# Setting the sign of converted float64 weights with one 16-bit and/or on the vector engine

## The chip, the core and the metric

The kernel runs on one core of a Trainium2 chip. The metric is device time in microseconds. The core has five engines with an instruction queue each: PE (matmul; its weight loads have a queue of their own in the profile, PEld), DVE (the vector engine), ACT (the scalar engine), POOL and SP. SP only issues DMAs here.

## The reference

Three stages follow each other on a batch of 2 with 768 positions: banded attention with 8 heads of 64, a token and channel mixer with skip connections, and a gated layer with a spatial mix.

```python
x = _attn_ref(...)                       # (2, 768, 512)
h = np.maximum(x.T @ w_tok1, 0.0) @ w_tok2          # per batch, over positions
u = x + h.T
x = u + np.maximum(u @ w_ch1, 0.0) @ w_ch2
h = np.maximum(x @ w_in, 0.0); u, v = split(h)
v = (v - mean(v)) / sqrt(var(v) + 1e-6)
y = (u * (w_spatial @ v + b_spatial)) @ w_out
```

All weights but `w_spatial` arrive as float64: a product of float32 draws with a numpy double.

## The kernel before

No engine reads float64, so the kernel loads the raw 8 bytes of each weight and rebuilds its value on the chip. That is done by `weight` (line 366), in blocks of 128 partitions by 512 weights. There are 42 such blocks: 6 for the token mixer (`tok_weights`, tile `wt`), 24 for the channel mixer (`ch_weight`, two for each of 12 slices `j`), 8 for `w_in` and 4 for `w_out` (`mlp2_weights`). `w_spatial` is float32 and takes a shorter way.

For each block the steps are these. Line 389 loads the block on SP's queue into a `raw` buffer, of which there are two. `mid` is a view of the middle 32 bits of each weight and `top` a view of its top 16 bits (sign, exponent and the first bits of the mantissa); both step by 8 bytes from one weight to the next. On ACT, line 390 copies `top` scaled by a power of two into the 16-bit tile `c` (its first half, `pw`), and line 391 writes the sign of `top` (1 or -1) into the second half of `c` (`sg`). On DVE, line 392 shifts the bits of `pw` by three and clears the sign bit, line 394 multiplies `pw` by `sg`, line 395 cuts `pw` to a power of two (`qq`), line 397 scales `mid` by `qq`, and line 399 adds `pw`. The result is split into a high part rounded to fp32r (line 400, a copy that either ACT or DVE may do) and a low rest (line 401, DVE). Every product of the mixers is then three fp32r matmuls (`mm3`, line 342).

The order of all instructions is made by `Plan` (line 98) when the kernel is built. Each operation names the engines on which it may run with an estimated cost (`act(n)`, `dve(n, x)`, where x is the number of elements per cycle that is assumed); the planner places the operation that can start first, among these the one with the longest chain behind it, and a copy goes to the engine on which it would end first, with a surcharge on busy engines. So a changed cost or a removed operation can change the order on every engine. Each queue then runs in the planned order.

Through attention the planner also places 80 matmuls on zeros (line 598), which occupy PE while it has nothing else. They are always 80, whatever else changes.

The attention groups (`group`, line 518) run scores on PE (line 484), bias and row minimum on DVE (line 501), the exponential on ACT (line 505), transposes on PE (line 511), copies out of PSUM (line 349) and the products with v (lines 539 and 549). The token mixer (`tok`, line 716) needs the `wt` blocks: the first three for its first product, the last three for its second, whose transposes are line 743. The channel mixer (`ch`, line 774) uses `w`, and its slices' weights stay resident for both batches.

Of the kernel before, what the change touches and what calls it, by code (L numbers as in the profile page):

```python
# [10 lines left out]
I16 = mybir.dt.int16  # L11
I32 = mybir.dt.int32
U32 = mybir.dt.uint32
AF = mybir.ActivationFunctionType
ALU = mybir.AluOpType
# [48 lines left out]
def f32(ap):  # L64
    return ap.bitcast(F32)
# [32 lines left out]
class Plan:  # L98
# [13 lines left out]
    def op(self, where, fn, reads=(), writes=(), pri=None, mode="full"):  # L112
        o = Op(where, fn, self.pri if pri is None else pri, len(self.ops))
        o.mode = mode if where[0][0] == "PE" else None
        o.plan, o.lam = self, self.lam
        for key in reads:
            w, r = self.seen.setdefault(key, [[], []])
            o.deps.update(w)
            r.append(o)
            if isinstance(key[0], Buf):  # L120
                key[0].users.append(o)
        for key in writes:
            w, r = self.seen.setdefault(key, [[], []])
            o.deps.update(r)
            o.deps.update(w)
            self.seen[key] = [[o], []]
            if isinstance(key[0], Buf):
                key[0].users.append(o)
                if key[0].first is None:
                    key[0].first = o  # L130
        o.deps.discard(o)
        self.ops.append(o)
        return o
# [65 lines left out]
def act(n, extra=0.0):  # L199
    return ("ACT", n / 1200 + 0.07 + extra)  # L200


def dve(n, x=1):
    return ("DVE", n * 0.00104 / x + 0.07)
# [6 lines left out]
def dma(nbytes):  # L211
    return ("SP", max(nbytes / 400e3, 0.5))
# [73 lines left out]
class Arm:  # L286
# [79 lines left out]
    def weight(self, hi, lo, src, hk, lk):  # L366

        op, n = self.plan.op, src.shape[-1]
        if src.dtype == F32:
            w = self.buf(self.stgp, "raw", [P, 1032], F32, 2)
            op([dma(P * n * 4)], lambda e: self.SY.dma_start(w()[:, :n], src), [], [(w,)])
            self.split(hi, lo, lambda: w()[:, :n], n, (w,), hk, lk)
            return
        w = self.buf(self.stgp, "raw", [P, 1032], I32, 2)
        c = self.buf(self.stgp, "c", [P, 1024], BF16, 2)  # L380
        q = self.buf(self.stgp, "q", [P, 512], BF16, 2)
        a = self.buf(self.stgp, "a", [P, 512], F32, 2)
        V = self.V
        mid = lambda: w()[:, 1:1 + 2 * n:2].bitcast(U32)
        top = lambda: w().bitcast(BF16)[:, 4:4 + 4 * n:4]
        pw, sg, qq = (lambda: c()[:, :n]), (lambda: c()[:, 512:512 + n]), (lambda: q()[:, :n])
        i16 = lambda x: x().bitcast(I16)
        aa = lambda: a()[:, :n]
        op([dma(P * n * 8)], lambda e: self.SY.dma_start(w().bitcast(I16)[:, 1:1 + 4 * n], src.bitcast(I16)), [], [(w,)], LDP)
        op([act(n)], lambda e: self.SC.mul(pw(), top(), 2.0 ** -112), [(w,)], [(c, 0)])  # L390
        op([act(n)], lambda e: self.SC.activation(sg(), top(), AF.Sign), [(w,)], [(c, 1)])  # L391
        op([dve(n, 2)], lambda e: V.tensor_scalar(
            out=i16(pw), in0=i16(pw), scalar1=3, scalar2=0x7FFF, op0=ALU.logical_shift_left, op1=ALU.bitwise_and), [], [(c, 0)])
        op([dve(n, 2)], lambda e: self.tt(e, pw(), pw(), sg(), ALU.mult), [(c, 1)], [(c, 0)])
        op([dve(n, 2)], lambda e: V.tensor_scalar(
            out=i16(qq), in0=i16(pw), scalar1=-128, scalar2=None, op0=ALU.bitwise_and), [(c, 0)], [(q,)])
        op([dve(n)], lambda e: V.scalar_tensor_tensor(  # L397
            out=aa(), in0=mid(), scalar=2.0 ** -36, in1=qq(), op0=ALU.mult, op1=ALU.mult), [(w,), (q,)], [(a,)])
        op([dve(n)], lambda e: self.tt(e, aa(), aa(), pw(), ALU.add), [(c, 0)], [(a,)])
        op(self.copies(n), lambda e: self.copy(e, hi(), aa()), [(a,)], [hk])  # L400
        op([dve(n)], lambda e: self.tt(e, lo(), aa(), f32(hi()), ALU.subtract), [(a,), hk], [lk])
# [645 lines left out]
```

## Time and profile before

| what | value |
|---|---|
| median of 3 runs | 476.6 us (476.33 to 477.08) |
| the profiled execution | 476.65 us |
| its span, first to last instruction | 474.9 us |
| outside the span | 1.75 us |
| PE busy | 469.1 us (99%) |
| PE weight loads busy | 414.3 us (87%) |
| DVE busy | 291.0 us (61%) |
| ACT busy | 210.3 us (44%) |

The busy share of an engine counts the time in which at least one of its instructions is under way. Matmuls overlap, and their ends are modelled, so short gaps between them can be covered. The weight loads are a second, stricter look at the same engine. Attention ends on PE at about 103 us, the token mixer's last part and the channel mixer of the first batch follow, the channel mixer of the second batch runs to about 336 us, and the gated layer fills the rest.

### The profile page before, as it was taken

How to read it: one execution, taken by the hardware profiler on the slowest of the kernel's cores; microseconds unless marked ns; L12 is line 12 of the kernel's file. 1: busy time of each engine (PE TensorE's matmuls, PEld its weight loads, DVE VectorE, ACT ScalarE, POOL GpSimd, SP SyncE). 2: the span in 40 equal slices, each digit the busy share in tenths (PEclk: the TensorE clock that was granted, in tenths of full speed). 3: DMA queues.
4: the chain of work that ended last, by engine and by line, in shares of the span. 5: the costliest groups of instructions: out<-in, count | busy, mean ns of one | idle time of the engine just before them, and what ended most of it. 6: DMA issues, size and time to landing. Idle time of an engine off the chain costs nothing.

```text
span 474.9 us, 8988 instructions
## 1 busy us (share of the span) xinstructions
PE 469.1 (99%) x3557; PEld 414.3 (87%) x3557; DVE 291.0 (61%) x781; ACT 210.3 (44%) x531; POOL 7.8 (2%) x17
## 2 busy tenths in 40 slices
PE   9999999999999999999999999999999999999996
PEld 5887888899988888888888888888999988899985
DVE  4899999979988787113977833247942503722520
ACT  5998899974645564101435311123612122411121
POOL 0111010000000000000000000000000000000000
PEclk9999999999999999999999999999999999999999
DMA  7955749223242433000043302110000021000012
GB/s 261 391 212 209 282 159 342 78 94 127 101 169 94 160 109 132 0 1 1 3 149 115 123 33 68 33 35 0 2 0 2 0 81 53 1 0 1 0 46 95
DMA packets 12000, 44.65 MB, mean 94 GB/s; under 512 B 1456, under 2 KB 1968, under 8 KB 10928
## 3 DMA queue, kind: packets, MB, share of 16 engines
q1 hardware_dynamic: 11952, 44.01, 26.0%
q8 instruction: 30, 0.49, 0.4%
q14 instruction: 18, 0.15, 0.1%
HBM read 40.86 MB, written 3.15 MB: 93 GB/s over the span
## 4 chain that ended last, share of the span: by engine, by line
PE 98%; DMA 1%; DVE 0%; issue 0%
PE p L344 27%; PE p L345 27%; PE p L346 27%; PE p L484 4%; PE p L511 4%; PE p L539 3%; PE p L598 2%; PE p L549 1%; DMA raw<-in_qkv 1%; PE p L743 1%; PE p L572 1%; PE dummy L259 1%; DVE c L349 0%; DVE zero L251 0%; DVE shift L253 0%
## 5 line engine op out<-in xcount | busy, mean ns | idle before, releaser
L344 PE MATMUL p<-raw,w 128*128 128x512 f32 (+1 forms) x192 | 64.8, 337 | 0.0
L345 PE MATMUL p<-raw,w 128*128 128x512 f32 (+1 forms) x192 | 64.7, 337 | 0.0
L346 PE MATMUL p<-raw,w 128*128 128x512 f32 (+1 forms) x192 | 64.6, 336 | 0.0
L790 ACT ACTIVATE raw<-p 128x512 fp32r<-128x512 f32 (+1 forms) x48 | 23.6, 491 | 85.1 <-PE p L346 78.3
L791 DVE SCALAR_TENSOR_TENSOR raw<-p,raw 128x512 fp32r<-128x512 f32 (+1 forms) x48 | 26.2, 554 | 35.4 <-ACT raw L790 35.0
L505 ACT ACTIVATE e<-e,nm 128x192 f32<-128x192 f32 (+1 forms) x96 | 42.4, 455 | 4.3 <-DVE nm L501 4.3
L346 PE MATMUL p<-uy1h,w 128*128 128x512 f32 (+2 forms) x128 | 43.2, 337 | 0.0
L346 PE MATMUL p<-uy0h,w 128*128 128x512 f32 (+2 forms) x128 | 43.2, 337 | 0.0
L345 PE MATMUL p<-uy1l,w 128*128 128x512 f32 (+2 forms) x128 | 43.1, 337 | 0.0
L345 PE MATMUL p<-uy0l,w 128*128 128x512 f32 (+2 forms) x128 | 43.1, 337 | 0.0
L344 PE MATMUL p<-uy1h,w 128*128 128x512 f32 (+2 forms) x128 | 43.1, 337 | 0.0
L344 PE MATMUL p<-uy0h,w 128*128 128x512 f32 (+2 forms) x128 | 43.1, 337 | 0.0
L390 ACT ACTIVATE c<-raw 128x512 bf16<-128x512 bf16 x42 | 28.6, 680 | 28.3 <-DMA raw<-in_w_in 12.6
L346 PEld LDWEIGHTS p<-raw,w 128*128 128x128 f32 x192 | 36.1, 188 | 4.2
L344 PEld LDWEIGHTS p<-raw,w 128*128 128x128 f32 x192 | 36.1, 188 | 4.1
L345 PEld LDWEIGHTS p<-raw,w 128*128 128x128 f32 x192 | 36.1, 188 | 4.0
L501 DVE CUSTOM_DVE_ANT_0 e<-p,bias 128x192 f32<-128x192 f32 (+1 forms) x96 | 27.5, 341 | 6.2 <-PE p L484 6.1
L397 DVE SCALAR_TENSOR_TENSOR a<-raw,q 128x512 f32<-128x512 uint32 x42 | 28.8, 686 | 0.4
L355 DVE TENSOR_TENSOR a<-a,c 128x512 f32<-128x512 f32 x42 | 28.8, 686 | 0.2
L391 ACT ACTIVATE c<-raw 128x512 bf16<-128x512 bf16 x42 | 28.3, 673 | 0.0
L355 DVE TENSOR_TENSOR w<-a,w 128x512 fp32r<-128x512 f32 x36 | 24.6, 685 | 2.8 <-ACT w L349 2.7
L355 DVE TENSOR_TENSOR c<-p,bsp 128x384 f32<-128x384 f32 x16 | 8.9, 558 | 28.1 <-PE p L346 28.1
(153 smaller groups left out, 1072.6 us busy)
## 6 DMA issues: line engine op xcount, KB each, us to landing
raw<-in_wch SPq DMA_DIRECT2D x24, 512.0 KB, 3.7
raw<-in_qkv SPq DMA_DIRECT2D x7, 1088.0 KB, 8.6
raw<-in_qkv SPq DMA_DIRECT2D x7, 848.0 KB, 6.3
raw<-in_w_in SPq DMA_DIRECT2D x8, 512.0 KB, 3.8
raw<-in_wt SPq DMA_DIRECT2D x6, 512.0 KB, 7.4
out<-a SPq DMA_DIRECT2D x11, 256.0 KB, 2.0
raw<-in_w_sp SPq DMA_DIRECT2D x6, 384.0 KB, 2.9
raw<-in_w_out SPq DMA_DIRECT2D x4, 512.0 KB, 3.9
```

The lines of the kernel that those rows point to most:

```text
L344: T.matmul(o, lhsT=w[0], rhs=x[0], start=first, stop=False)
L345: T.matmul(o, lhsT=w[0], rhs=x[1], start=False, stop=False)
L346: T.matmul(o, lhsT=w[1], rhs=x[0], start=False, stop=last)
L355: self.eng[e].tensor_tensor(out=o, in0=a, in1=b, op=op)
L390: op([act(n)], lambda e: self.SC.mul(pw(), top(), 2.0 ** -112), [(w,)], [(c, 0)])
L391: op([act(n)], lambda e: self.SC.activation(sg(), top(), AF.Sign), [(w,)], [(c, 1)])
L397: op([dve(n)], lambda e: V.scalar_tensor_tensor(out=aa(), in0=mid(), scalar=2.0 ** -36, in1=qq(), op0=ALU.mult, op1=ALU.mult), [(w,), (q,) ...
L484: T.matmul(banks[k][i]()[x * D:x * D + D, o:o + w], lhsT=r[:, q0:q0 + D], rhs=r[:, k0:k0 + w], start=True, stop=True)
L501: op([dve(w)], lambda e, j=j, o=o, w=w, bs=bs: V.tensor_tensor_reduce(out=e_()[:, o:o + w], in0=s()[:, o:o + w], in1=bias()[:, bs], scale= ...
L505: op([act(w, 0.2)], lambda e, j=j, o=o, w=w: SC.activation(e_()[:, o:o + w], e_()[:, o:o + w], AF.Exp, bias=nm()[:, j:j + 1], scale=-1.0, ...
L790: op([act(n)], lambda e, m=m, r=r, sl=sl, n=n: SC.activation(r()[:, 0, sl], m()[:, :n], AF.Relu), [(m,)], [(r, z, 0)])
L791: op([dve(n)], lambda e, m=m, r=r, sl=sl, n=n: V.scalar_tensor_tensor(out=r()[:, 1, sl], in0=m()[:, :n], scalar=0.0, in1=f32(r()[:, 0, sl] ...
```

## The change

The sign is no longer computed on ACT. Line 391 (Sign, ACT) and line 394 (16-bit multiplication, DVE) go. One DVE instruction takes their place: it masks the sign bit of `top` and joins it to `pw` with an or, both as 16-bit integers. Its first input is the strided view `top`, so it reads the `raw` buffer. The planner is told one element per cycle for it (`dve(n)`), where the multiplication stood with two (`dve(n, 2)`). The second half of `c` is not used any more.

```diff
-        pw, sg, qq = (lambda: c()[:, :n]), (lambda: c()[:, 512:512 + n]), (lambda: q()[:, :n])
+        pw, qq = (lambda: c()[:, :n]), (lambda: q()[:, :n])
         i16 = lambda x: x().bitcast(I16)
         aa = lambda: a()[:, :n]
         op([dma(P * n * 8)], lambda e: self.SY.dma_start(w().bitcast(I16)[:, 1:1 + 4 * n], src.bitcast(I16)), [], [(w,)], LDP)
         op([act(n)], lambda e: self.SC.mul(pw(), top(), 2.0 ** -112), [(w,)], [(c, 0)])
-        op([act(n)], lambda e: self.SC.activation(sg(), top(), AF.Sign), [(w,)], [(c, 1)])
         op([dve(n, 2)], lambda e: V.tensor_scalar(
             out=i16(pw), in0=i16(pw), scalar1=3, scalar2=0x7FFF, op0=ALU.logical_shift_left, op1=ALU.bitwise_and), [], [(c, 0)])
-        op([dve(n, 2)], lambda e: self.tt(e, pw(), pw(), sg(), ALU.mult), [(c, 1)], [(c, 0)])
+        op([dve(n)], lambda e: V.scalar_tensor_tensor(
+            out=i16(pw), in0=top().bitcast(I16), scalar=-32768, in1=i16(pw), op0=ALU.bitwise_and, op1=ALU.bitwise_or), [(w,)], [(c, 0)])
         op([dve(n, 2)], lambda e: V.tensor_scalar(
             out=i16(qq), in0=i16(pw), scalar1=-128, scalar2=None, op0=ALU.bitwise_and), [(c, 0)], [(q,)])
```

## Rows read from the trace of the kernel before

**Rows 1.** The page's first lines and its clock row (40 slices of the span):
```profile
span 474.9 us, 8988 instructions
PE 469.1 (99%) x3557; PEld 414.3 (87%) x3557; DVE 291.0 (61%) x781; ACT 210.3 (44%) x531; POOL 7.8 (2%) x17
...
PEclk9999999999999999999999999999999999999999
```

**Rows 2.** Busy time by stretch: from:to and length, engines, clock, DMA share, GB/s:
```profile
5.00:47.00 42.00, 41.64 (x675) 33.17 (x673) 35.40 (x159) 38.37 (x139) 5.45 (x9) 1.00 0.75 283
47.00:107.00 60.00, 59.51 (x855) 53.31 (x856) 56.00 (x207) 54.31 (x174) 2.14 (x4) 1.00 0.52 191
107.00:190.00 83.00, 83.00 (x488) 73.74 (x487) 69.50 (x151) 44.21 (x80) 0.00 (x0) 1.00 0.38 128
...
230.00:280.00 50.00, 50.00 (x289) 43.72 (x288) 38.75 (x80) 19.03 (x35) 0.00 (x0) 1.00 0.30 100
280.00:470.00 190.00, 190.00 (x1012) 173.41 (x1011) 77.12 (x150) 46.13 (x89) 0.00 (x0) 1.00 0.07 24
```
The engines stand in the order PE, PEld, DVE, ACT, POOL, each with its number of instructions.

**Rows 3.** The chain that ended last, shares of the span by engine (page, 4):
```profile
PE 98%; DMA 1%; DVE 0%; issue 0%
```

**Rows 4.** Groups of instructions by line: busy us, mean ns of one, idle before them:
```profile
L391 ACT ACTIVATE c<-raw 128x512 bf16<-128x512 bf16 x42 | 28.3, 673 | 0.0
L355 DVE TENSOR_TENSOR c<-c 128x512 bf16<-128x512 bf16 x42 | 17.9, 425 | 2.0 <-ACT c L391 1.7
L397 DVE SCALAR_TENSOR_TENSOR a<-raw,q 128x512 f32<-128x512 uint32 x42 | 28.8, 686 | 0.4
L355 DVE TENSOR_TENSOR a<-a,c 128x512 f32<-128x512 f32 x42 | 28.8, 686 | 0.2
```

**Rows 5.** Line 391 alone by stretch: ACT busy, instructions, clock, DMA, GB/s:
```profile
5.00:47.00 42.00, 3.44 (x5) 1.00 0.75 283
47.00:107.00 60.00, 6.30 (x9) 1.00 0.52 191
107.00:190.00 83.00, 13.21 (x20) 1.00 0.38 128
...
230.00:280.00 50.00, 5.30 (x8) 1.00 0.30 100
```

**Rows 6.** Groups by line, 47 to 107 us: the DVE's casts of converted blocks:
```profile
L349 DVE CAST w<-a 128x512 fp32r<-128x512 f32 x4 | 1.7, 418 | 0.0
L349 DVE CAST wth<-a 128x512 fp32r<-128x512 f32 x3 | 1.3, 419 | 0.0
```

**Rows 7.** Groups by line, 5 to 107 us: PE's weight loads and fill:
```profile
L511 PEld LDWEIGHTS p<-ident,e 128*128 128x128 f32 x144 | 15.9, 140 | 4.3 <-ACT pt L349 1.2 <-ACT e L505 1.1 <-ACT ct L349 0.6
L484 PEld LDWEIGHTS p<-raw 64*64 64x64 f32 x336 | 11.0, 132 | 3.7 <-DMA raw<-in_qkv 0.8 <-PE p L572 0.6 <-PE p L511 0.5
...
L598 PE MATMUL p<-zero 128*128 128x256 bf16 x80 | 12.4, 277 | 0.1
```

**Rows 8.** Who waited for whom, 107 to 190 us: total us, times, longest:
```profile
ACT w L349 <- DVE a L355: 14.5, 12, 1.5
...
DVE c L355 <- ACT c L391: 1.2, 5, 0.3
```

**Rows 9.** Timeline around the token mixer's sixth block: start, us, engine, line:
```profile
60.85 0.68 DVE L355 TENSOR_TENSOR wtl<-a,wth 128x512 fp32r<-128x512 f32 x1
...
61.05 0.49 PE L743 MATMUL p<-ident,xp 128*128 128x128 f32 x3
...
61.55 0.33 PE L345 MATMUL p<-wtl,hh 128*128 128x384 f32 x1
```

**Rows 10.** Timeline: PE's longest idle time in attention, before a score group:
```profile
47.49 0.78 PE L484 MATMUL p<-raw 64*64 64x128 f32 x16 [0.62 <-DMA raw<-in_qkv]
```

**Rows 11.** Timeline: both blocks of channel slice 2 written; the slice's first matmul:
```profile
105.91 1.29 DVE L355 TENSOR_TENSOR w<-a,w 128x512 fp32r<-128x512 f32 x2
...
122.32 0.39 PE L344 MATMUL p<-uy0h,w 128*128 128x512 f32 x1
```

## The prediction

> **What bounds the kernel now.** I read the busy shares first. PE is busy for 469.1 of 474.9 us, and its granted clock is full in every slice, so no clock level is to be won or lost [rows 1]. Then I read the chain that ended last: 98% of it is PE [rows 3]. A busy PE can hide gaps, since matmul ends are modelled, so I went on to busy time by stretch [rows 2], cut where the work changes: the first part of attention (5 to 47 us), attention with the token mixer (47 to 107), the channel mixer with most weight conversions (107 to 190), the conversions for the gated layer (230 to 280), and what follows. In the last three PE is busy for the whole stretch while DVE has 13.5, 11.3 and 112.9 us to spare. In the first two PE is still busy for all but 0.36 and 0.49 us, but DVE (35.4 of 42, 56.0 of 60) and ACT (38.4 of 42, 54.3 of 60) are nearly full as well. These are the only stretches in which the two engines that the change touches could set PE's pace.
>
> How much idle time can PE be hiding there? Its weight loads are the stricter measure. They are busy for 73.74 of 83 us, 0.89, in the stretch from 107 to 190, where PE has no gap at all; 0.89 (53.31 of 60) from 47 to 107; and 0.79 (33.17 of 42) from 5 to 47 [rows 2]. If 0.89 is what a full PE looks like, the first stretch hides about 0.1 x 42 = 4.2 us and the second about none. Shapes differ between stretches, so that is an estimate. In the first stretch PE also runs the 80 matmuls on zeros [rows 7]: their number is fixed, so they are work that no faster engine removes.
>
> The Trainium skill (Trainium Kernel Development and Optimization, section Performance Expectations) calls matmul busy time a bad metric because matmuls are pipelined, and wants weight-load busy time read instead. By the first, 99% leaves nothing to gain; by the second, 87% leaves something. The trace sides with the page for the stretch up to 47 us and shows no difference between the second and the third.
>
> **The change part by part.**
>
> *Line 391 goes from ACT.* 42 x 673 ns = 28.3 us of ACT work [rows 4]. By stretch it is 3.44, 6.30, 13.21 and 5.30 us [rows 5]. In the last two ACT is busy for 44.2 of 83 and 19.0 of 50 us, so there the removal is worth nothing: PE is full, and ACT itself waits for DVE (the high cast waited 14.5 us in total for the sum on DVE) [rows 2, 8]. In the first two it takes 9.7 us off an ACT that is busy for 92.7 of 102 us.
>
> *Line 394 becomes the and/or on DVE.* The multiplication takes 425 ns [rows 4]. The trace has no 16-bit and/or with two sources. Its nearest row is line 397: the same instruction kind, the same 512 elements, a first input that steps by 8 bytes in the same buffer, a 16-bit second one: 686 ns [rows 4]. The other end is 425 ns, if the 16-bit form ran as fast as the multiplication that it replaces. I take 686, since the stride is what the two share. So each block costs DVE 0 to 0.26 us more, and I take 0.26: 5 x 0.26 = 1.3 us from 5 to 47, 9 x 0.26 = 2.3 from 47 to 107, 20 x 0.26 = 5.2 from 107 to 190, 8 x 0.26 = 2.1 from 230 to 280; 42 x 0.26 = 11 us in all. DVE's idle time in these stretches is 6.6, 4.0, 13.5 and 11.3 us [rows 2], so it stays under full in each: 36.7 of 42, 58.3 of 60, 74.7 of 83, 40.9 of 50.
>
> The DVE's microarchitecture page of the Trainium skill (Vector Engine (DVE) Microarchitecture Reference, section 5.2) speaks against the change: a source that hops at every element streams at 1.73 ns per column plus about 75 ns, which for 512 columns gives 0.96 us as an estimate, and 0.54 us more per block. This trace disagrees for line 397, which hops by 8 bytes and takes 686 ns, exactly as long as the sum of line 399 without a hop [rows 4].
>
> *What gives DVE the room back.* From 47 to 107 us DVE also does seven casts of high parts (4 and 3, 418 and 419 ns) that may run on either engine [rows 6]. With ACT relieved of 6.3 us there, the planner can move them: up to 7 x 0.42 = 2.9 us off DVE, against the 2.3 us added. If it moves none, DVE keeps 1.7 us of idle time in 60; that is the thin place.
>
> *Waits.* The DVE's wait for the Sign goes (1.2 us from 107 to 190 [rows 8]); late next is line 392's input from line 390, which is untouched. The new instruction waits for the `raw` buffer's load, which line 390 has waited for already, so no new wait stands in DVE's queue. The `raw` buffer is given back by line 397, as before, now 0.26 us later in a block's chain; behind that on SP stand the next weight loads and attention's loads. A conversion that ends later matters only if PE is near it. For the channel slices it is not: slice 2, with the smallest lead, is written by 107.2 and first used at 122.32 [rows 11]; 14 blocks at 0.26 us make it at most 3.7 us later, and the lead stays above 11 us.
>
> *The sum.* 0 us from 107 us on, since PE is full and the weights lead. Before that, a gain or loss only through PE's small waits. The waits that ACT ends at the transposes (line 511) are 1.2 + 1.1 + 0.6 = 2.9 us [rows 7]; these can shrink. PE's longest wait, 0.62 us, is for a load of attention's own and stays [rows 10]. Against this stands the longer DVE chain. The balance is a few tenths down: the profiled execution's 476.65 becomes about 476.4. Its span of 474.9 plus 1.75 us outside is that 476.65, 0.05 above the median of 476.6, so the same number serves for both.
>
> **The rivals.**
>
> *Faster: ACT was pacing attention.* For it: ACT is 91% busy over the first 102 us, and transposes wait for it. Against it: the idle time is partly filled by the fixed matmuls on zeros, so a shorter chain only moves them. If half of the 2.9 us goes the time is 475.2; if all of it, 473.8; an outer bound is the 4.2 us of hidden idle time, 472.5.
>
> *Slower: the sixth token block comes late.* The last low part of `wt` runs from 60.85 to 61.53; PE starts the transposes of the token mixer's second product at 61.05 and the matmul that reads that low part at 61.55 [rows 9]. There is no lead. Six blocks with 0.26 us more each make it 1.6 us later if DVE, which has little room there, does not take the casts off. From the point where PE has no other product ready at 61 us, it waits: 476.65 + 1.6 = 478.2. Against it: the planner knows the longer cost and has attention work to put ahead.
>
> *The order alone.* Removing 42 operations and changing 42 costs lets the planner reorder everything up to 107 us, with no trend. The transposes' weight loads have 4.3 us of idle time in front and the scores' 3.7 [rows 7]; an eighth of these 8 us either way is 1.0 us: 475.6 to 477.6. This mixes into all the cases.
>
> *The change does not do what it says:* the and/or costs DVE nothing (425 ns). Then the slower case falls away and the time is as forecast, 476.4. By the page's 0.96 us per instruction the stretch from 47 to 107 would need 9 x 0.54 = 4.9 us more of a DVE with 4.0 idle. As a mechanism of this kernel, a DVE that is full there delays attention by what does not fit: 56.0 + 4.9 - 60 = 0.9 us, 477.5, unless the casts move. I give it 0.03, within the slower case, because the row of line 397 contradicts it.
>
> **How the numbers follow.** About 0.2% (0.95 us) is what a measurement of this kernel can tell from no change. PE full with waits that cancel (the forecast, the cheap and/or with it): 0.45. Faster, ACT's relief: 0.30. Slower, DVE's chain: 0.25, of which 0.03 is the page's. The range must leave out no more than a fifth: downwards it stops just above the full 2.9 us at 474.0, leaving out the hidden 4.2 us; upwards it takes the 478.2 of the late block and half a microsecond of order on top, 478.8. The likeliest case's own range is 475.6 to 477.6.
>
> **What would show it.** The new DVE row should read close to 686 ns and line 391 should be gone. From 47 to 107 us ACT should lose some 3 to 6 us and DVE stay within 1.5 us of its 56.0, with fewer of the seven casts on DVE. PE should be busy without a gap from 107 us on, and the weight loads from 5 to 107 us keep their idle time to within a microsecond. The forecast is wrong if the idle time at the transposes shrinks by more than a microsecond without appearing elsewhere, if the first matmul of the token mixer's second product waits for `wtl`, or if the channel mixer starts more than 1 us earlier or later than now.

## The result and the profile after

The changed kernel takes 482.7 us (481.68 to 483.42) against 476.8 (476.33 to 477.08): 1.0107 times as long, 95% interval 1.0087 to 1.0127. (The quotient of the two medians is a little larger, 1.0123; shares below go by the ratio.) The profiled execution took 482.98 us, its span is 481.1 us, 6.2 longer than before [rows 1]. The page's first lines, its clock row and its chain of work that ended last, after:

```profile
span 481.1 us, 8908 instructions
...
PE 472.4 (98%) x3557; PEld 416.9 (87%) x3557; DVE 300.9 (63%) x778; ACT 190.8 (40%) x492; POOL 6.9 (1%) x17
...
PEclk9999979999999999999999999999999999999999
...
PE 90%; DMA 3%; DVE 3%; ACT 2%; issue 1%; ACTq 0%; DVEq 0%
```

ACT lost 19.5 us of work and DVE gained 9.9, as the change says; three copies moved from DVE to ACT (DVE 781 to 778 instructions, ACT 531 to 492 with 42 Signs gone). But one slice of the clock row now reads 7, and the chain, 98% PE before [rows 3], holds DMA, DVE and ACT. The price of the new instruction isn't the reason. The groups by line, after (line 393 is the and/or, line 397 the unchanged scaling of `mid`):

```profile
L393 DVE SCALAR_TENSOR_TENSOR c<-raw,c 128x512 int16<-128x512 int16 x42 | 28.9, 688 | 0.3
L397 DVE SCALAR_TENSOR_TENSOR a<-raw,q 128x512 f32<-128x512 uint32 x42 | 28.8, 686 | 0.3
```

Where the time went shows in the busy time by stretch, after (from:to and length; PE, PEld, DVE, ACT, POOL; clock, DMA share, GB/s), beside [rows 2]:

```profile
5.00:47.00 42.00, 41.67 (x654) 33.84 (x654) 34.73 (x155) 37.97 (x137) 4.53 (x9) 1.00 0.72 272
47.00:107.00 60.00, 56.58 (x795) 49.50 (x797) 53.26 (x195) 47.99 (x160) 2.14 (x4) 0.94 0.51 183
107.00:190.00 83.00, 83.00 (x545) 74.17 (x540) 73.72 (x148) 34.77 (x65) 0.00 (x0) 1.00 0.37 127
230.00:280.00 50.00, 50.00 (x288) 43.73 (x288) 44.58 (x88) 15.09 (x26) 0.00 (x0) 1.00 0.27 87
...
280.00:470.00 190.00, 190.00 (x1013) 173.42 (x1012) 80.33 (x156) 45.95 (x89) 0.00 (x0) 1.00 0.07 24
```

From 107 us on PE is full, as before. Only the second stretch is worse: PE is busy for 56.58 us where it was busy for 59.51, and the mean clock is 0.94. A landmark, one product found in both traces, confirms that all of the loss lies early. The first product of the channel mixer for the second batch starts here, before and then after:

```profile
210.17 0.39 PE L344 MATMUL p<-uy1h,w 128*128 128x512 f32 x1
```

```profile
216.36 0.39 PE L344 MATMUL p<-uy1h,w 128*128 128x512 f32 x1
```

From it to the end of the span both kernels take 264.7 us (474.9 - 210.17 and 481.1 - 216.36). The 6.2 us were all lost before it. This is the place, in the timeline after (start, duration, engine, line, [idle before <- what ended it]):

```profile
57.47 0.63 ACT L730 ACTIVATE hh<-p 128x256 fp32r<-128x256 f32 x2
...
60.78 0.65 ACT L390 ACTIVATE c<-raw 128x512 bf16<-128x512 bf16 x1 [2.69 <-DMA raw<-in_wch]
61.34 0.35 ACT L349 COPY ct<-p 128x256 f32<-128x256 f32 x1
...
61.75 0.69 PE L572 MATMUL p<-ident,ct 128*128 128x128 f32 x2 [2.60 <-ACT ct L349]
...
62.37 1.56 PE L484 MATMUL p<-raw 64*64 64x192 f32 x16
```

ACT waits 2.69 us for the load of the seventh weight block, the first of the channel mixer. Behind that step in ACT's queue stands the copy `ct` of attention, and PE needs it: 2.60 us idle. In the kernel before ACT came to the same step after that copy, at a time when the block was there:

```profile
61.99 0.72 ACT L390 ACTIVATE c<-raw 128x512 bf16<-128x512 bf16 x1
```

SP issued the load at 51.49 us, hardly later than before (51.32), behind two loads of attention. The DMA issues from 48 to 56 us give KB and us from issue to landing, before and then after:

```profile
raw<-in_qkv SPq DMA_DIRECT2D x1, 1088.0 KB, 8.8
raw<-in_qkv SPq DMA_DIRECT2D x1, 848.0 KB, 6.5
raw<-in_wch SPq DMA_DIRECT2D x1, 512.0 KB, 8.1
```

```profile
raw<-in_qkv SPq DMA_DIRECT2D x1, 1088.0 KB, 9.8
raw<-in_qkv SPq DMA_DIRECT2D x1, 848.0 KB, 7.5
raw<-in_wch SPq DMA_DIRECT2D x1, 512.0 KB, 9.3
```

So it landed at about 59.4 us before and 60.8 after, while ACT was ready for it at 58.1 (60.78 - 2.69). About half of ACT's wait is thus a load that landed 1.4 us later; with the landing of before it would have been some 1.3 us. Why the three loads took longer isn't shown. As this idle time ended, PE's clock fell to half, 1.2 of 2.4 GHz. Busy time after, cut there:

```profile
57.00:61.30 4.30, 2.15 (x46) 1.84 (x46) 3.04 (x14) 1.61 (x7) 0.00 (x0) 1.00 0.49 165
61.31:68.14 6.83, 6.39 (x35) 5.11 (x35) 4.83 (x18) 6.09 (x21) 0.00 (x0) 0.50 0.02 7
68.20:72.00 3.80, 3.80 (x80) 3.39 (x80) 3.12 (x15) 2.82 (x10) 0.45 (x1) 1.00 0.30 63
```

The sum of the loss: PE is busy for 2.9 us less from 47 to 107 us (59.51 - 56.58), and the 6.39 us of work at half clock would take 3.2 us less at full. Together 6.1 of the 6.2 us. In the trace that accounts for the time. Whether the order or the new work made it so is what the experiments were for.

### The profile page after: what moved, and what is told of

Its sections match the earlier page's. It is cut to its first block, busy times and chain, and to the rows that moved or that the text cites. A ratio compares the mean times of both kernels' runs of the same rounds, so it can differ in the third digit from the quotient of the medians.

```text
span 481.1 us, 8908 instructions
## 1 busy us (share of the span) xinstructions
PE 472.4 (98%) x3557; PEld 416.9 (87%) x3557; DVE 300.9 (63%) x778; ACT 190.8 (40%) x492; POOL 6.9 (1%) x17
## 4 chain that ended last, share of the span: by engine, by line
PE 90%; DMA 3%; DVE 3%; ACT 2%; issue 1%; ACTq 0%; DVEq 0%
PE p L344 26%; PE p L345 26%; PE p L346 26%; DMA raw<-in_wch 3%; PE p L484 3%; PE p L511 3%; PE p L598 2%; PE p L539 2%; PE p L549 1%; PE p L572 1%; PE p L743 1%; ACT e L505 1%; PE dummy L259 1%; DVE xl L355 1%; DVE e L501 0%
## 5 line engine op out<-in xcount | busy, mean ns | idle before, releaser
L390 ACT ACTIVATE c<-raw 128x512 bf16<-128x512 bf16 x42 | 28.2, 674 | 33.9 <-DMA raw<-in_w_in 15.3
L393 DVE SCALAR_TENSOR_TENSOR c<-raw,c 128x512 int16<-128x512 int16 x42 | 28.9, 688 | 0.3
L345 PEld LDWEIGHTS p<-uy1l,w 128*128 128x128 f32 x128 | 24.1, 188 | 2.3
```

The lines of the kernel that those rows point to most:

```text
L345: T.matmul(o, lhsT=w[0], rhs=x[1], start=False, stop=False)
L393: op([dve(n)], lambda e: V.scalar_tensor_tensor(out=i16(pw), in0=top().bitcast(I16), scalar=-32768, in1=i16(pw), op0=ALU.bitwise_and, op1= ...
```

## The experiments

The *cost* theory: the and/or makes each block's DVE chain longer, and that costs the time. The *order* theory: the planner, told other work, emitted another order, and in that order ACT met a load that was not there. The planned orders of the two kernels differ on PE, ACT and DVE: from 5 to 47 us, for one, PE runs 675 matmuls before [rows 2] and 654 after. Ratios are to the kernel before, run beside each experiment, with 95% intervals; they are not the quotients of the medians, from which they differ by up to 0.16 percentage points.

**The new work in the old order.** The and/or runs on the chip, but the planner still counts a Sign (which issues nothing) and the old cost. Against the changed kernel:

```diff
         op([act(n)], lambda e: self.SC.mul(pw(), top(), 2.0 ** -112), [(w,)], [(c, 0)])
+        op([act(n)], lambda e: None, [(w,)], [(c, 1)])
...
-        op([dve(n)], lambda e: V.scalar_tensor_tensor(
-            out=i16(pw), in0=top().bitcast(I16), scalar=-32768, in1=i16(pw), op0=ALU.bitwise_and, op1=ALU.bitwise_or), [(w,)], [(c, 0)])
+        op([dve(n, 2)], lambda e: V.scalar_tensor_tensor(
+            out=i16(pw), in0=top().bitcast(I16), scalar=-32768, in1=i16(pw), op0=ALU.bitwise_and, op1=ALU.bitwise_or), [(c, 1)], [(c, 0)])
```

> The and/or is executed, but the planner still counts a Sign on ACT and the half-cost multiplication, so every queue keeps the order of the kernel before, with the Sign left out and the and/or in the multiplication's place. Order theory (the loss comes from one conversion step placed ahead of attention's copies on ACT, where it waits for its load, and from the halved clock behind that): no such wait here, 476.0 to 477.6 us, granted clock full from 7 to 470 us. Cost theory (the and/or takes 688 ns on DVE where the multiplication took 425, and DVE paces PE before 107 us): 480 us or more, with PE's idle time spread over 47 to 107 us.

Measured: 478.4 against 477.7 us, 1.0021 (1.0007 to 1.0034). Clock full, span 476.6 us. Its busy time by stretch, and the group of its and/or (line 394 here):

```profile
47.00:107.00 60.00, 58.73 (x870) 52.21 (x865) 57.10 (x207) 49.34 (x163) 2.15 (x4) 1.00 0.56 200
107.00:190.00 83.00, 83.00 (x489) 73.90 (x488) 74.47 (x152) 34.68 (x62) 0.00 (x0) 1.00 0.37 127
```

```profile
L394 DVE SCALAR_TENSOR_TENSOR c<-raw,c 128x512 int16<-128x512 int16 x42 | 29.0, 691 | 0.3
```

All the new work costs 0.2%, about a fifth of the loss. DVE rises to 57.1 of 60 us, yet PE shows no wait for it: its longest, before 107 us, is 1.0 us for a load of attention's, where it was 0.62 [rows 10].

**The old work in the new order.** The Sign is issued in the same step as the scaled copy, and the multiplication stands where the and/or stands, at its planned cost.

```diff
-        op([act(n)], lambda e: self.SC.mul(pw(), top(), 2.0 ** -112), [(w,)], [(c, 0)])
-        op([act(n)], lambda e: self.SC.activation(sg(), top(), AF.Sign), [(w,)], [(c, 1)])
+        op([act(n)], lambda e: (self.SC.mul(pw(), top(), 2.0 ** -112), self.SC.activation(sg(), top(), AF.Sign)), [(w,)], [(c, 0)])
...
-        op([dve(n, 2)], lambda e: self.tt(e, pw(), pw(), sg(), ALU.mult), [(c, 1)], [(c, 0)])
+        op([dve(n)], lambda e: self.tt(e, pw(), pw(), sg(), ALU.mult), [(w,)], [(c, 0)])
```

> The converse: the planner counts as in the changed kernel, so the queues keep its order, but the Sign is executed on ACT right behind the scaled copy, and the multiplication stands in the place of the and/or. Order theory: the wait on ACT near 58 to 61 us is there, PE stands idle 2 to 3.5 us, the clock halves behind it, 481.5 to 485 us (the Sign's 0.6 us may add to the wait of the copies behind it). Cost theory: 476 to 478 us.

Measured: 484.7 us, 1.0163 (1.0136 to 1.0190). The same wait at the same step (timeline), and then a fall of the clock to half (busy time):

```profile
61.73 1.19 ACT L390 ACTIVATE c<-raw 128x512 bf16<-128x512 bf16 x2 [2.04 <-DMA raw<-in_wch]
...
63.24 0.44 PE L571 MATMUL p<-ident,ct 128*128 128x128 f32 x2 [3.14 <-ACT ct L349]
```

```profile
65.19:68.60 3.41, 2.96 (x12) 2.96 (x13) 2.73 (x13) 3.41 (x10) 0.00 (x0) 0.50 0.00 0
```

With these two the cost theory falls: the new work in the old order costs 0.2%, the old work in the new order 1.6%. The 0.6% that it costs beyond the changed kernel goes with the Sign, which now doubles that ACT step (1.19 us for 0.65); that this is all of it isn't shown.

**That one step, four places later.** The changed kernel, with the seventh block's scaled copy put behind the next four ACT instructions after planning; all else in its order.

```diff
+        for i, (o, e) in enumerate(out):
+            if getattr(o, "shift", 0):
...
+                out.insert(j, out.pop(i))
...
-        op([act(n)], lambda e: self.SC.mul(pw(), top(), 2.0 ** -112), [(w,)], [(c, 0)])
+        o = op([act(n)], lambda e: self.SC.mul(pw(), top(), 2.0 ** -112), [(w,)], [(c, 0)])
+        self.blocks = getattr(self, "blocks", 0) + 1
+        o.shift = 4 if self.banded and self.blocks == 7 else 0
```

> The changed kernel with one instruction moved: the seventh block's scaled copy on ACT (the one that waits 2.69 us for its load) goes behind the next four attention instructions of ACT (a copy, two exponentials, a copy). All else keeps its place. Order theory: PE's idle time of 2.6 us at that place is gone and the clock does not fall, so 476.3 to 477.8 us. If only the idle time counted and the clock fell for another reason, 480 us. Cost theory: 482.7 us as the changed kernel.

Measured: 480.1 us, 1.0057 (1.0031 to 1.0083), with the clock full in the trace; of the other four executions one reads a mean of 0.996. The order theory's 476.3 to 477.8 us is missed: moving one instruction of 0.65 us takes back 0.50% of the 1.07, some 2.4 us, and not all. PE's longest waits in this order are others (timeline; line 398 is the scaled copy, line 521 the transposes, line 494 the scores):

```profile
61.24 0.67 ACT L398 ACTIVATE c<-raw 128x512 bf16<-128x512 bf16 x1 [0.69 <-DMA raw<-in_wch]
...
63.16 0.55 PE L521 MATMUL p<-ident,e 128*128 128x128 f32 x3 [1.67 <-ACT e L515]
...
73.57 0.77 PE L494 MATMUL p<-raw 64*64 64x128 f32 x16 [1.23 <-DVE first L589]
```

**The same step earlier, in the kernel before.** As above, `shift = -11`.

> The kernel before with one instruction moved: the seventh block's scaled copy on ACT goes 11 places ahead, between the two copies of the token mixer's hidden tile, to about 57.8 us, where its load (it landed at 59.45 us) is not there yet. Old work throughout. Order theory: ACT waits about 1.6 us and PE goes idle for 1 to 2 us; 478 us if the clock holds, 480 to 481.5 if it halves for some 6 us as in the changed kernel. Cost theory: 476.8 us, as PE has other work.

Measured: 479.7 us, 1.0057 (1.0026 to 1.0089). In the profiled execution, 479.0 us, ACT waits 1.11 us for the load, PE 1.50 behind it, and the clock is full. But the six executions fall into two groups. Three took 478.7 to 479.0 us at a mean granted clock of 0.998 to 1.000. Three took 480.3 to 481.6 us at 0.996, which is also the reading of all four executions of the long wait below, whose trace holds 3.41 us of half clock. So one and the same order ran with the clock full or, by this reading, with a stretch at half clock, and the means of the two groups lie 2.2 us apart. Where the clock fell in the three no trace shows. By the ratio, one ACT step in the wrong place makes the old order lose half of what the change lost.

**What a wait of PE costs.** In the kernel before, one product at about 178 us is preceded by a matmul on zeros that adds nothing and waits for a chain of small DVE operations: 4 in the first run, 14 in the second. PE is otherwise full there, and the order stays.

```diff
+                        if (b, j, kk, n) == (0, 6, 2, 256):
+                            x, zr = self.late, self.zero
+                            V.tensor_scalar(out=x, in0=m()[:, :128], scalar1=0.0, scalar2=None, op0=ALU.mult)
+                            for _ in range(3):      # 13 in the second run
+                                V.tensor_scalar(out=x, in0=x, scalar1=0.0, scalar2=None, op0=ALU.mult)
+                            T.matmul(..., lhsT=x.bitcast(BF16)[:, :P], rhs=zr, start=False, stop=False)
```

> What a stall of PE costs by itself. The kernel before, with one forced wait in a stretch where PE is full and everything else has time (channel slice 6 of the first batch, near 150 us): four dependent small DVE operations read the bank that PE has just finished, and PE's next matmul reads their result (it adds zeros). Some 0.8 us of PE idle time. If a stall costs its own length alone: about 0.8 us over the kernel before, clock full throughout.

> The same with fourteen dependent DVE operations: some 2.5 to 3 us of PE idle time, as long as the wait of 2.6 us in the changed kernel. If idle time alone counts: 2.5 to 3 us over the kernel before, so about 480 us. If an idle time of that length makes the clock fall, as the rows of the changed kernel show it behind theirs (half speed from 61.3 to 68.1 us): the same plus about 3 us, about 483 us, with a stretch at half clock behind the stall.

Measured: 479.3 us, 1.0035 (1.0017 to 1.0054), and 482.6 us, 1.0103 (1.0082 to 1.0125), against 477.8. The short wait is 1.21 us and costs 1.5, at full clock. The long one is 3.82 us and costs 4.9. Its timeline:

```profile
180.32 0.76 PE L345 MATMUL p<-raw,w 128*128 128x512 f32 x1 [3.82 <-DVE late L793]
180.88 0.63 PE L346 MATMUL p<-raw,w 128*128 128x512 f32 x1
...
184.38 0.39 PE L346 MATMUL p<-uy0l,w 128*128 128x512 f32 x1
```

The busy time behind it:

```profile
180.57:183.98 3.41, 3.41 (x9) 2.65 (x9) 3.25 (x8) 0.62 (x1) 0.00 (x0) 0.50 0.21 71
```

A matmul of 512 columns reads 0.63 us in that stretch and 0.39 after it. All four executions read a mean clock of 0.996. By this a wait brings the half clock in an order that is otherwise unchanged. It costs 3.41 / 2 = 1.7 us of PE time, so wait and clock add up to 5.5 us in the profiled execution, 0.6 above what the medians show.

**The wait filled.** The changed kernel with 22 matmuls on zeros put ahead of the transpose that waits, so that PE works through the wait. They are extra work, and no result depends on them.

```diff
+                self.backs = getattr(self, "backs", 0) + 1
+                if self.backs == 13:
+                    s = next(x for x in self.plan.slots["p2"] if x.tile is None)
+                    for _ in range(22):
+                        T.matmul(s()[:, :2 * P], lhsT=self.zero, rhs=self.zero[:, 0:1].broadcast_to([P, 2 * P]), start=True, stop=True)
                 for k in range(2):
                     T.transpose(c()[:, (2 + k) * P:(3 + k) * P], ct()[:, j, k * P:(k + 1) * P], self.ident)
```

> The changed kernel, with 22 matmuls on zeros (about 2.4 us of PE's time) put on PE's queue just before the transpose that waits for ACT at 61.75 us. They write a bank that is free then and is overwritten by the next scores. The wait of ACT for its load and all orders stay; PE is active through it. If the half clock is a part of the loss of its own: no half clock near 61 to 68 us, and the changed kernel's 482.7 us fall by about 3 us, to 479 to 480.5. If the loss is the wait alone: 482.7 us or a little more.

Measured: 481.2 us (479.27 to 483.38), 1.0076 (1.0046 to 1.0107), span 480.0, clock 1.00 throughout. The fill and the wait beside it (timeline):

```profile
58.58 2.62 PE L575 MATMUL p<-zero 128*128 128x256 bf16 x22
60.36 0.66 ACT L390 ACTIVATE c<-raw 128x512 bf16<-128x512 bf16 x1 [2.71 <-DMA raw<-in_wch]
61.33 0.44 PE L577 MATMUL p<-ident,ct 128*128 128x128 f32 x2
```

ACT's wait is unchanged and the clock stays full, yet the profiled execution is only 1.1 us shorter, not 3.2. The median is 1.5 us lower, with intervals that overlap, so that the fill gains anything isn't clear of the noise. PE, at full clock, comes to new waits behind it: beside the 2.62 us of zeros it now stands idle for 0.66 us before a transpose and 0.51 before another. What came back with the full clock is a third to a half of what the clock's row suggests.

**Loads planned later.** The changed kernel, with the planner told that a load takes longer (`LAG["SP"]` 2.1 to 4.5 us), so that no step is placed ahead of its data.

> The changed kernel, with the planner told that data lands 4.5 us after a transfer's planned end instead of 2.1 (the seventh block's load took 9.28 us from issue to landing). The steps that wait for loads are then placed later among attention's work. Order theory: fewer or shorter waits of ACT for loads before 107 us, no half clock, 476.5 to 480 us. Cost theory: 482 to 483 us.

Measured: 482.9 us, 1.0100 (1.0080 to 1.0120), as slow as the change. By itself this is the time that the cost theory forecast, and the order theory's 476.5 to 480 us is missed; what tells the two apart are the first two experiments. No ACT step waits for a weight load before 107 us, and the clock is full. PE's longest waits in this order (who waited for whom: total us, times, longest):

```profile
PE p L484 <- DVE nm L501: 1.1, 2, 0.7
...
PE p L743 <- DVE hl L731: 0.7, 1, 0.7
PE p L346 <- DVE hl L731: 0.5, 1, 0.5
PE p L539 <- DVE first L579: 0.5, 2, 0.3
PE p L484 <- PE p L511: 0.5, 1, 0.5
```

They add up to 3.3 us, and from 5 to 140 us PE is busy for 3.0 us less than before (131.1 and 134.2 of 135). The span is 6.5 us longer than that of the kernel before, so these rows place only about half of the loss. The late load is thus a way in which the changed kernel's order loses time, and not the only way in which an order can. I had taken that one wait for the whole cause; this run doesn't allow it.

**Three more orders.** If almost any other order is worse than the one that the kernel had, then small changes of planned costs should cost time with the old work too. The first run has the new work with the and/or planned at half its cost, `dve(n, 2)`. The other two have the old work, once with the multiplication planned at full cost, `dve(n)`, and once with 3 ns more in the planner's fixed cost of every ACT instruction.

```diff
-    return ("ACT", n / 1200 + 0.07 + extra)
+    return ("ACT", n / 1200 + 0.073 + extra)
```

> The changed kernel's work, but the planner is told that the and/or takes half the time (as the multiplication had). Only costs differ, so this is a third order of the same instructions; the conversions' first steps stand at other places among attention's copies on ACT. Order theory: the time follows the waits of these steps for their loads and PE's idle time behind them, and can fall anywhere from 476.5 to 484 us; PE's idle times over 0.25 us plus half of the time at half clock account for the difference to the kernel before within 1.5 us. Cost theory: 482.7 us, as the work is that of the changed kernel.

> No change of work at all: the Sign and the multiplication of the kernel before, but the planner is told the full cost for the multiplication. Only the order of the same instructions changes, as much as in the changed kernel. Order theory, widened (the order of the kernel before is an unusually good one, and nearly any other costs PE waits before 107 us): 478.5 to 484 us. If the changed kernel's order was bad by a single accident: 476.5 to 478 us.

> No change of work: the kernel before with the planner's fixed cost of an ACT instruction at 73 instead of 70 ns, a change that means nothing on the chip. Widened order theory: the order differs and the time rises by 1 to 6 us, 478.5 to 483. Accident theory: 476.5 to 478 us.

Measured, with the other orders beside them:

| work | order | ratio | interval |
|---|---|---|---|
| new | of the kernel before | 1.0021 | 1.0007 to 1.0034 |
| old | mult at full cost | 1.0018 | 1.0004 to 1.0032 |
| new | and/or at half cost | 1.0039 | 1.0025 to 1.0053 |
| old | ACT plus 3 ns | 1.0046 | 1.0028 to 1.0064 |
| new | one step later | 1.0057 | 1.0031 to 1.0083 |
| old | one step earlier | 1.0057 | 1.0026 to 1.0089 |
| new | loads later | 1.0100 | 1.0080 to 1.0120 |
| new | of the change | 1.0107 | 1.0087 to 1.0127 |
| old | of the change | 1.0163 | 1.0136 to 1.0190 |

All seven other orders measured slower than the old one, by 0.2 to 1.6%. Rows with new work hold its 0.2% too; without it the order of the and/or at half cost is only 0.18% worse, with intervals that overlap, so that one isn't shown to be worse. The 478.4 us of the multiplication at full cost lie between the two forecasts. The clearest case is the last: three nanoseconds in a planned cost, which add no work to any engine, are worth 0.5%, and its profile shows no single cause, but two waits of PE of 1.0 us each for attention's loads. No version beats the kernel before.

## Why the prediction was wrong

**The step that failed is the size of "the order alone".** It was put at 1.0 us either way, as an eighth of the idle time in front of the transposes' and the scores' weight loads [rows 7]. That eighth had no row behind it. The runs show the seven other orders 0.9 to 7.8 us slower (0.18 to 1.63% of 477), never a gain; the same new work cost 0.2% in the old order and 1.07% in the new one, so by the difference the order is worth some 0.9%, 4 us. It was also put as a trend-free term mixed into every case, where the old order was one with hardly a wait left: PE's longest was 0.62 us [rows 10]. From there a change of order can lose much and win little. The 98% of PE in the chain [rows 3] was read as safety.

**"No clock level is to be won or lost" failed.** A full clock in every slice [rows 1] says that nothing is to be won. It doesn't say that nothing can be lost: in the profiled executions half clock came with waits of PE of 2.60 us (the change), 3.14 and 3.82 us, and not with those of 1.67, 1.50 and 1.21 us. No sharp line follows from this: in the order with the wait of 1.50 us, three of six executions read the lower clock.

**"Waits" looked at the wrong queue.** It asked whether the new instruction adds a wait to DVE's queue, and it was right that it doesn't. It called line 390 untouched. In the code it is. But in the new order line 390 of the seventh block stands ahead of attention's copy, right behind `hh`, and the wait stood in ACT's queue. That the planner put it there because the Sign is gone isn't shown: with the old work and only the multiplication's planned cost changed, it stands right behind `hh` too, but at a time when the load was there (timeline):

```profile
62.65 0.42 ACT L730 ACTIVATE hh<-p 128x256 fp32r<-128x256 f32 x1
62.92 0.73 ACT L390 ACTIVATE c<-raw 128x512 bf16<-128x512 bf16 x1
```

The load's place was in the trace of the kernel before: issued at 51.32 us, 8.1 us to landing, and read by ACT at 61.99.

**The rivals.** None had this mechanism. The slower one, the sixth token block, did not happen: before 107 us PE waits for no `wtl` (who waited for whom, PE, 5 to 107 us, after):

```profile
PE p L572 <- ACT ct L349: 2.6, 1, 2.6
PE p L484 <- DMA raw<-in_qkv: 0.3, 1, 0.3
PE p L511 <- ACT pt L349: 0.3, 1, 0.3
PE p L743 <- DVE uy0l L355: 0.2, 1, 0.2
```

The faster one, that ACT paced attention, is not borne out: from 47 to 107 us ACT lost 6.3 us in the new order and 5.0 in the old one (the first experiment, 49.34 of 54.31), and PE gained nothing in either.

**What held.** The and/or takes 688 ns, where line 397's 686 was chosen over 425. The row of the Trainium skill behind the prediction's 0.96 us (Vector Engine (DVE) Microarchitecture Reference, section 5.2) was measured with a source that hops 4 KiB at every element. This trace disagrees with the estimate from it for a 16-bit source that steps by 8 bytes. DVE gained 9.9 us in all (11 forecast) and is full in no stretch. ACT lost what was forecast, a little over the mark (6.3 us from 47 to 107, the mark 3 to 6). PE is busy without a gap from 107 us on, and from the second batch's channel mixer to the end both kernels take 264.7 us. The prediction's own marks caught the failure: the channel mixer was not to start over 1 us later, and it starts at 109.51 us, not 102.95; the weight loads were to keep their idle time before 107 us within a microsecond, and from 47 to 107 alone they are busy for 49.50 us instead of 53.31; DVE was to stay within 1.5 us of its 56.0 there, and is busy for 53.26.

**What stays open.** How the 6.2 us divide. The waits and the half clock add up to them in the trace, but filling the wait gave back only 1.1 us in the profile, and moving the step some 2.4 by the ratios. That the order costs most of the loss is shown; which of its waits cost how much isn't, nor why the order with the loads later is as slow. A move of the same step behind attention's next copies, together with the two later ones that wait, was not tried.

## What to carry to other kernels

Where a planner makes the order, a change is two changes: what it runs, and the order that its costs bring about. Run the new work in the old order and the old work in the new order before anything is said of an instruction's price; here they came out at +0.2% and +1.6%. A kernel whose bounding engine hardly waits sits on an order that was found, so an edit to planned costs can lose time there: here 0.2 to 1.0% in six other orders, and 1.6% in the changed order with the old work. Look at each step that waits for a load: what stands behind it in its engine's queue waits too, as attention's copy did here.

## What the runs showed of the hardware

In the profiled executions half clock came with PE waits of 2.6 to 3.8 us, from 0.4 us before the wait's end (the change) to 1.95 us after it (the old work in the new order). It lasted for 3.41 us twice and for 6.83 us in the changed kernel. A matmul of 512 columns then reads 0.63 us for 0.39. In three traces the same load took longer the closer it was issued behind two others: 512 KB took 8.1 us (before) and 9.3 us (after) when SP issued them 2.5 and 2.2 us behind 1,936 KB of attention's, and 4.8 us in the order with the multiplication at full cost, where the distance was 5.9 us. The median of all 24 such loads before is 3.7 us:

```profile
raw<-in_wch SPq DMA_DIRECT2D x24, 512.0 KB, 3.7
```

A 16-bit and/or with two sources, one of them stepping by 8 bytes, takes as long on DVE as line 397, whose first source is 32-bit with the same step: 688 and 686 ns for 512 elements of a partition.
